# Zero products on TensorE at launch, and a gate and its stores divided once more in the last tile

## The chip, the cores and the metric

One core of one Trainium2 chip. The metric is the time of the whole kernel on the device, in microseconds (us), as the median of several executions. "Granted clock" is the mean TensorE clock in an execution's clock records, 1.0 being full; the time before the first record (19.21 us in the profiled run of before) is counted as full. In these traces TensorE multiplies matrices into PSUM, VectorE and ScalarE work on the products element by element, and SyncE only issues DMA transfers. I call the "clock gate" open where a clock record says 1.0 and shut where it says 0.5; the same product of 128 columns starts every 107 ns before the first record of before and every 55 ns after it.

## The reference

```python
# x: (8, 3072, 256) float32
X = np.fft.rfft(x, axis=1)                       # along the sequence
Yr = Xr @ w_r - Xi @ w_i + b_r                   # complex 256 x 256 product
Yi = Xr @ w_i + Xi @ w_r + b_i
Yr = np.sign(Yr) * np.maximum(np.abs(Yr) - 0.01, 0.0)   # the same for Yi
y = np.fft.irfft(Yr + 1j * Yi, n=3072, axis=1)
# then a channel mix on y, with y_prev = y moved by one token
xk = mu_k * y + (1 - mu_k) * y_prev
xr = mu_r * y + (1 - mu_r) * y_prev
k = np.maximum(xk @ w_k, 0.0)                    # 256 -> 1024
v = k * k @ w_v                                  # 1024 -> 256
out = v / (1 + np.exp(-(xr @ w_r2)))             # the gate
```

## The kernel before

The transforms are done as matrix products. A small scheduler in the kernel's own Python issues everything in an order fixed at build time, and PSUM is four pairs of banks that go round (`take`, `release`). The 8 x 3072 tokens of the channel mix are 48 tiles of 512.

The launch: the first sequence comes in four chunks; `direct` does the first DFT step on each as it lands (L326 in the profile), and `turn` the transposes after it (L344).

```python
def load_x(b, q):
    t = xs_pool.tile([N1, 8, D], BF16, name="xs")
    src = x[b].rearrange("(n1 n2) d -> n1 n2 d", n2=N2)
    nc.gpsimd.dma_start(out=t, in_=src[:, 8 * q:8 * q + 8, :])
    xs[b, q] = t
...
def take():
    f, i = min((f, i) for i, f in enumerate(pair_free) if f is not None)
    pair_free[i] = None
    return banks[:, i, :], i
...
# direct(), chunk q, half c
for i in range(8):
    nc.tensor.matmul(pv[:, i, :], xt[:, i, 128 * c:128 * c + 128], FT, start=True, stop=True)
...
# turn(u)
for i in range(4):
    for c in range(NCD):
        nc.tensor.matmul(ps[:, 256 * i + 128 * c:256 * i + 128 * c + 128],
                         live["X1"][:, c, 4 * u + i].rearrange("p r n -> p (r n)"), ident, ...)
```

The end: the last tile's products (L670), its gate (L681) and its four stores (L692), done in two parts. Every second store of the last tile goes by ScalarE's queue, all others by SyncE's.

```python
            lo, hi = (512 * p, 512 * p + 512) if final else (0, 1024)

            def gated(k):
                nc.vector.tensor_tensor(out=o[:, lo:hi], in0=ps[:, lo:hi], in1=rg[:, lo:hi], op=ALU.mult)
                ...
            def store(k):
                ...
                for xx in range(4):
                    queue = nc.scalar if final and xx % 2 else nc.sync
                    queue.dma_start(out=rows[hh, half, xx][:, lo:hi], in_=o[32 * xx:32 * xx + 32, lo:hi])
```

## Time and profile before

| | before |
|---|---|
| median of 3 runs | 592.51 us (592.41 to 592.64) |
| profiled run, its span | 592.85 us, 591.0 us |
| TensorE busy | 566.1 us (96%) |
| VectorE, ScalarE busy | 522.4 us (88%), 421.0 us (71%) |
| last weight load of TensorE to the span's end | 5.35 us |

### The profile page before, as it was taken

What the parts mean: (1) busy time and instruction counts of PE and PEld (TensorE: products, weight loads), DVE (VectorE), ACT (ScalarE), POOL (GpSimd) and SP (SyncE); (2) the same over time, 40 slices, a digit from 0 to 9 for tenths busy, and PEclk for the clock granted to TensorE, in tenths of its full rate; (3) what the DMA queues carried; (4) which work ended last, traced back from release to release, by engine and by line L of the source; (5) the groups of instructions that cost most, each with busy time, mean ns of one, the idle gap of its engine ahead of it and who ended that gap; (6) DMA issues with size and microseconds to landing.
All of it is one profiled execution on the core that took longest, in us unless ns stands there. A gap on an engine that the chain in (4) does not pass through costs nothing.

```text
span 591.0 us, 12301 instructions
## 1 busy us (share of the span) xinstructions
PE 566.1 (96%) x4822; PEld 429.1 (73%) x4889; DVE 522.4 (88%) x831; ACT 421.0 (71%) x459; POOL 26.7 (5%) x56
## 2 busy tenths in 40 slices
PE   3999999999999999999999999999999999999996
PEld 3888666777767777677777777677876787776665
DVE  7799999789998899898998989988999889979883
ACT  5786967677768677676777677777776867767652
POOL 7101000000000000000000000000000000000000
PEclk9999999999999999999999999999999999999999
DMA  8976978724598265963478655683337722352223
GB/s 134 142 149 161 187 181 231 179 72 106 127 230 234 60 139 143 248 182 78 107 183 245 148 116 130 169 229 107 101 97 232 179 55 73 104 165 71 65 57 94
DMA packets 69594, 84.38 MB, mean 143 GB/s; under 512 B 9121, under 2 KB 54560, under 8 KB 69536
## 3 DMA queue, kind: packets, MB, share of 16 engines
q1 hardware_dynamic: 62912, 68.98, 41.7%
q0 software_dynamic: 6432, 14.36, 16.7%
q8 instruction: 38, 0.62, 0.4%
q10 hardware_dynamic: 192, 0.26, 0.2%
q14 instruction: 20, 0.16, 0.1%
HBM read 50.73 MB, written 47.19 MB: 166 GB/s over the span
## 4 chain that ended last, share of the span: by engine, by line
PE 84%; ACT 6%; DVE 4%; issue 2%; DMA 2%; POOL 0%; SPq 0%; DVEq 0%; POOLq 0%; ACTq 0%
PE banks L670 28%; PE banks L626 24%; PE banks L414 14%; PE banks L653 5%; PE banks L453 4%; PE banks L271 3%; PE banks L386 3%; ACT rl L632 3%; PE banks L534 2%; ACT rg L658 2%; DMA xs<-in_x_dram 1%; PE banks L344 1%; DVE YT L220 1%; DMA out_dram<-o 1%; DVE z L426 1%
## 5 line engine op out<-in xcount | busy, mean ns | idle before, releaser
L632 ACT ACTIVATE rl<-banks 128x1024 bf16<-128x1024 f32 x192 | 193.6, 1029 | 94.3 <-PE banks L626 88.5
L626 PE MATMUL banks<-xk,wk 128*128 128x512 bf16 x701 | 188.7, 379 | 5.3 <-DVE xk L599 0.7
L670 PE MATMUL banks<-wv,k 128*128 128x256 bf16 x1536 | 183.0, 272 | 0.4 <-ACT rl L632 0.3
L670 PEld LDWEIGHTS <-k 128*128 128x128 bf16 x1536 | 149.3, 98 | 29.1 <-issue 1.4
L638 DVE TENSOR_TENSOR k<-rl 128x1024 bf16<-128x1024 bf16 x192 | 130.3, 684 | 13.6 <-ACT rl L632 13.5
L626 PEld LDWEIGHTS <-wk 128*128 128x128 bf16 x768 | 73.9, 98 | 60.7 <-issue 3.1
L414 PEld LDWEIGHTS <-XT 128*128 128x128 bf16 x768 | 74.5, 98 | 16.1 <-DVE XT L396 0.7
L414 PE MATMUL banks<-wi,XT 128*128 128x256 bf16 x384 | 73.3, 273 | 0.1
L414 PE MATMUL banks<-wr,XT 128*128 128x256 bf16 x384 | 73.3, 272 | 0.1
L599 DVE SCALAR_TENSOR_TENSOR xk<-diff,muk,YT 128x512 bf16<-128x512 bf16 x96 | 69.0, 744 | 0.2
L599 DVE SCALAR_TENSOR_TENSOR xr<-diff,mur,YT 128x512 bf16<-128x512 bf16 x96 | 68.7, 744 | 0.0
L681 DVE TENSOR_TENSOR o<-banks,rg 128x1024 f32<-128x1024 f32 (+1 forms) x49 | 58.6, 1195 | 3.7 <-PE banks L670 3.4
L218 ACT ACTIVATE YT<-banks 128x768 bf16<-128x768 f32 x57 | 43.5, 830 | 11.3 <-PE banks L534 7.9
L218 ACT ACTIVATE XT<-banks 128x1024 bf16<-128x1024 f32 (+2 forms) x46 | 43.3, 950 | 10.4 <-PE banks L386 10.4
L653 PE MATMUL banks<-wrm,xr 128*128 128x256 bf16 x384 | 49.8, 272 | 0.1
L658 ACT ACTIVATE rg<-banks 128x1024 bf16<-128x1024 f32 x48 | 49.2, 1025 | 0.0
L431 ACT ACTIVATE z<-banks 128x1024 bf16<-128x1024 f32 x32 | 32.7, 1022 | 19.7 <-PE banks L414 19.6
L653 PEld LDWEIGHTS <-xr 128*128 128x128 bf16 x384 | 37.2, 98 | 11.6 <-issue 0.2
L218 ACT ACTIVATE V<-banks 128x1024 bf16<-128x1024 f32 x35 | 35.9, 1025 | 12.8 <-PE banks L453 12.8
L218 ACT ACTIVATE A<-banks 96x1024 bf16<-96x1024 f32 (+1 forms) x39 | 39.3, 1023 | 7.5 <-PE banks L271 6.2
L593 DVE TENSOR_TENSOR diff<-YT 128x1024 bf16<-128x1024 bf16 x48 | 32.8, 683 | 3.8 <-ACT YT L218 3.8
L220 DVE CAST A<-banks 96x1024 bf16<-96x1024 f32 (+1 forms) x21 | 25.5, 1221 | 11.4 <-PE banks L271 9.4
(90 smaller groups left out, 448.3 us busy)
## 6 DMA issues: line engine op xcount, KB each, us to landing
out_dram<-o SPq DMA_DIRECT2D x188, 128.0 KB, 2.3
xs<-in_x_dram POOLq DMA_DIRECT2D x32, 384.0 KB, 6.5
Vdr<-V SPq DMA_DIRECT2D x192, 64.0 KB, 1.8
V<-Vdr SPq DMA_DIRECT2D x32, 384.0 KB, 7.0
Adr<-A SPq DMA_DIRECT2D x24, 384.0 KB, 5.6
A<-Adr SPq DMA_DIRECT2D x48, 192.0 KB, 4.3
wk<-in_moe_w_k_dram POOLq DMA_DIRECT2D x1, 512.0 KB, 14.1
wv<-in_moe_w_v_dram POOLq DMA_DIRECT2D x1, 512.0 KB, 14.5
```

Of the source, the lines that this page charges most:

```text
L218: nc.scalar.activation(out, in_, AF.Copy, bias=0.0, scale=1.0)
L414: nc.tensor.matmul(o, lhs, w[:, c, :], start=(w is wr and c == 0), stop=(w is wi and c == NCD - 1))
L431: nc.scalar.activation(z, ps, AF.Copy, bias=0.0, scale=1.0)
L593: nc.vector.tensor_tensor(out=df, in0=y, in1=yp, op=ALU.subtract)
L599: nc.vector.scalar_tensor_tensor(out=m[:, c, :], in0=df[:, c, :], scalar=mu[:, c:c + 1], in1=yp[:, c, :], op0=ALU.mult, op1=ALU.add)
L626: nc.tensor.matmul(ps[:, 512 * f:512 * f + 512], wk[:, c, 128 * ff:128 * ff + 128], xk[:, c, :], start=(c == 0), stop=(c == NCD - 1))
L632: nc.scalar.activation(rl, ps, AF.Relu, bias=0.0, scale=1.0)
L638: nc.vector.tensor_tensor(out=k2, in0=rl, in1=rl, op=ALU.mult)
L653: nc.tensor.matmul(ps[:, 256 * q:256 * q + 256], xr[:, c, 128 * q:128 * q + 128], wrm[:, c, :], start=(c == 0), stop=(c == NCD - 1))
L658: nc.scalar.activation(rg, ps, AF.Sigmoid, bias=0.0, scale=1.0)
L670: nc.tensor.matmul(ps[:, 256 * q:256 * q + 256], K2[t][:, ff, 128 * q:128 * q + 128], wv[:, ff, :], start=(ff == 0), stop=(ff == NCF - 1))
L681: nc.vector.tensor_tensor(out=o[:, lo:hi], in0=ps[:, lo:hi], in1=rg[:, lo:hi], op=ALU.mult)
```

## The change

Its intent: TensorE waits for inputs until 6.3 us anyway, so let it multiply zeros in that time, so that its clock gate is open when the first real products come; a few more zero products between the chunks are to keep it open. And at the end, gate and store the last 512 columns as twice 256, so that the last stores start earlier.

```diff
+    idle = const.tile([128, 512], BF16, name="idle")
+    nc.vector.memset(idle, 0.0)
+
+    def keep_warm(ps, n):
+        for _ in range(n):
+            nc.tensor.matmul(ps[:, 0:512], idle[:, 0:128], idle, start=True, stop=True)
@@ direct(), after a chunk's products
+                if b == 0 and c == 1:
+                    spare, i = take()
+                    keep_warm(spare, 2 if q < 3 else 1)
+                    release(i, end + 0.5)
@@ v_unit()
-            lo, hi = (512 * p, 512 * p + 512) if final else (0, 1024)
+            cuts = ((0, 512), (512, 768, 1024))[p] if final else (0, 1024)
             def gated(k):
-                nc.vector.tensor_tensor(out=o[:, lo:hi], in0=ps[:, lo:hi], in1=rg[:, lo:hi], op=ALU.mult)
-                e = run_on("dve", k, 0.7 if final else 1.22)
+                for lo, hi in zip(cuts, cuts[1:]):
+                    nc.vector.tensor_tensor(out=o[:, lo:hi], in0=ps[:, lo:hi], in1=rg[:, lo:hi], op=ALU.mult)
+                    e = run_on("dve", k, 1.22 * (hi - lo) / 1024)
+                    if final:
+                        store(lo, hi)
@@ before the first unit is issued
+    spare, i = take()
+    keep_warm(spare, 14)
+    release(i, 6.0)
```

(Cut: the tiles before the last store as they did.) That is 21 zero products, one memset, one gate and four stores more.

## The prediction

> **What bounds the kernel now.** I read the page first (busy time, then the chain that ended last), then the launch and the end, where the change acts: groups by shape and the order of time for the launch; order of time, waits and landings for the end.
>
> ```profile
> PE 566.1 (96%) x4822; PEld 429.1 (73%) x4889; DVE 522.4 (88%) x831; ACT 421.0 (71%) x459; POOL 26.7 (5%) x56
> ...
> PEclk9999999999999999999999999999999999999999
> ...
> PE 84%; ACT 6%; DVE 4%; issue 2%; DMA 2%; POOL 0%; SPq 0%; DVEq 0%; POOLq 0%; ACTq 0%
> ```
>
> TensorE is busy for 96% of the span and makes up 84% of the chain; the body (from some 25 us to 584 us) gets no instruction from the change. What is left is a launch of some 25 us and an end of some 7 us. The clock row shows full clock everywhere, also at launch. The durations contradict it. Groups by shape, 6 to 20 us, then 20 to 60 us:
>
> ```profile
> L326 PE MATMUL banks<-FT,xs 96*128 96x96 f16 x64 | 5.9, 280 | 2.0 <-DMA xs<-in_x_dram 2.0
> L344 PE MATMUL banks<-ident,YT 128*128 128x128 f16 x48 | 4.9, 289 | 0.8 <-ACT YT L218 0.7
> ```
>
> ```profile
> L326 PE MATMUL banks<-FT,xs 96*128 96x96 f16 x64 | 3.6, 205 | 0.5 <-ACT V L218 0.4
> L344 PE MATMUL banks<-ident,YT 128*128 128x128 f16 x48 | 3.2, 219 | 0.6 <-DVE YT L220 0.6
> ```
>
> The same products take 280 and 289 ns at launch, 205 and 219 ns later. The starts show it too: L344 starts every 107 ns between 15.35 and 19 us, every 55 ns later; L326 every 80 ns, later every 43 ns. The first clock record in the trace stands at 19.2 us (to full); before it the page assumes full clock. So the launch runs at half clock until 19.2 us. The launch in order of time:
>
> ```profile
> 12.64 1.58 ACT L735 ACTIVATE G<-YT,sc 128x1536 f16<-128x1536 f32 x1
> 12.77 1.46 PE L326 MATMUL banks<-FT,xs 96*128 96x96 f16 x16 [0.33 <-DMA xs<-in_x_dram]
> ...
> 14.34 0.96 DVE L220 CAST YT<-banks 128x768 bf16<-128x768 f32 x1 [0.83 <-PE banks L326]
> ...
> 14.81 1.56 ACT L739 ACTIVATE G<-YT,sc 128x1536 f16<-128x1536 f32 x1
> ...
> 17.17 1.94 ACT L218 ACTIVATE A<-banks 128x1024 bf16<-128x1024 f32 x2 [0.80 <-PE banks L344]
> ...
> 19.56 1.02 ACT L218 ACTIVATE A<-banks 128x1024 bf16<-128x1024 f32 x1 [0.45 <-PE banks L344]
> ```
>
> L326 waits for the loads of x (9.11, 10.98 and 12.77 us), which a faster TensorE cannot move. After L344, ScalarE waits twice for TensorE: 0.80 and 0.45 us. The end, in order of time and in the queue's own waits:
>
> ```profile
> 585.15 2.59 ACTq L692 DMA_DIRECT2D out_dram<-o  x4
> 586.12 0.69 DVE L681 TENSOR_TENSOR o<-banks,rg 128x512 f32<-128x512 f32 x1 [1.00 <-PE banks L670]
> ```
>
> ```profile
> SPq L692 <- DMA out_dram<-o: 1.5, 2, 1.3
> ```
>
> The last gate ends at 586.81, but the last store starts only at 588.35 and lands at 590.12; 0.9 us of closing barrier follow. In between the SyncE queue waits 1.3 us for a store to land. The end is therefore set by the store queue, not by the gate.
>
> [...] L344 was dense from 15.35, and the gate opened at 19.2. [...] no trace here has zero operands yet. [...] the built program lets the first quarter gate wait for the same last product as before. [...] here one store costs its queue 0.36 to 0.47 us, which matters when seven queue up.
>
> **The change part by part.** The listing of both built programs shows pure additions: 21 zero products and their weight loads, one memset first on VectorE, one gate more, four stores more. Everything else keeps its order; PSUM pairs only rotate by one.
>
> *Launch, the added products.* 14 products of 512 columns at half clock take some 14 x 427 ns = 6.0 us (512 columns at L344's 128 columns in 107 ns), from about 1.1 us (VectorE is idle until 2.36, so the memset is free) to at most 7.1. If the gate opens on the way, they end before 6.3, when the first real product can start. In the worst case x's first chunk is 0.8 us late, which the wait until 9.11 for the second swallows. The later 2+2+2+1 cost 0.43 us a pair at full clock and lie in the waits for x or ahead of L344.
>
> *Launch, the gain.* Step by step:
> - Third and fourth chunk of L326 still start at 10.98 and 12.77. ScalarE cannot use the gain: L735 waits for VectorE's angles (end 12.60), so L735, the copy at 14.12 and L739 (to 16.37) keep their times. VectorE's copy of the last part starts at 13.65 instead of 14.34 and ends at 14.61.
> - L344 starts at 14.96 and is not held at 15.35. At 55 ns its units of 8 end at 15.57, 16.00, 16.44; then PSUM pairs must come free.
> - ScalarE's A copies now follow L739 back to back: 16.28, 17.20, 18.12 instead of 17.17, 18.09, 19.56. The next, XT0, starts at 19.06 instead of 20.48: **1.4 us** earlier. VectorE (16.83 first copy, four small G pieces, then 17.2 and 18.4) keeps up.
> - From there ScalarE is the chain: XT 19.54, GI 20.28 (was 21.65), VectorE's L396 at about 22.0 (was 23.37), L414 at 22.3 instead of 23.69. Its weights landed by 14.2, the bias at 21.8, ahead of its use at 23.6. The next loads of x, used at 34, landed by 32.3. So the 1.4 us go through to the body, which is a chain of relative times.
>
> *End, the gates.* 1024 columns take 1224 ns and 512 take 692, so 256 take about 160 + 266 = 426 ns. The first quarter is ready at 586.54 (0.27 earlier), the second at 586.97 (0.16 later).
>
> *End, the stores.* Each store takes the next of eight completion semaphores and waits until that one's previous store has landed. In the kernel before, SyncE's second store of part 0 shares one with ScalarE's first store of part 0 (issued 585.15, landed 587.51): it started at 587.53, then 587.94, 588.35. With four stores more the numbering shifts. In the new listing it is already the fourth store of the tile before (old start 585.17, without a wait) that shares with ScalarE's first one. So SyncE stands from 585.1 until that lands, at about 587.2 (estimate: 15 of its 16 parts landed by 587.03, the last at 587.51 beside the store that now waits), and then has **seven** stores to issue instead of three: 0.36 + 5 x 0.43 = 2.5 us to the last start at 589.7, landing some 1.65 later at 591.3 instead of 590.12. The end grows by about **1.2 us** (0.9 if the landing comes at 587.0 and issue is quick, 1.5 if at 587.5).
>
> *Sum.* 592.5 - 1.4 + 1.2 = 592.3 us.
>
> **The rivals.**
> - *The end gains as intended.* If the semaphores don't bind as I read the listing, finer stores overlap better, and the end changes by 0 to -0.4: about 590.9. Against: the 1.3 us wait is measured, and the listing names the same kind of wait one store earlier. I give this 15%.
> - *Zero products don't open the gate, or it closes in the waits for x.* Then the launch gains nothing and the end's loss stays: 593.7. For: no trace has zeros. Against: the waits are at most 1.5 us, and the gate closed at the very end only after a window with 0.3 us of work. 12%.
> - *The launch's gain is eaten later*, by loads at fixed times or by VectorE: 593 to 593.7. Against: each load has 1.7 us or more to spare. 8%.
>
> **Range and chances.** The body cancels and runs scatter by 0.2 us. The launch's part is -1.4 with 0.25 either way, the end's +1.2 with 0.35, together about 0.45; the rivals stretch both sides to 590.9 and 593.7. Centre 592.3, range 590.9 to 593.5. Two per cent are 11.9 us; neither end of the kernel has that much: 0.01, 0.98, 0.01.
>
> **What would show it right or wrong.** L344 at launch at 219 ns a product, with the second start right after 14.96; ScalarE's first A copy at 16.3 and XT0 near 19.1; L414 near 22.3; the last product of TensorE about 1.4 us earlier. Then the time from the last product to the span's end 1.2 us longer than now (586.1 to 591.0, 4.9 us), SyncE waiting some 2 us for a store with seven stores behind. Wrong: L344 still at 289 ns (gate shut); the last product moves by less than 1 us (gain eaten); the time after the last product stays at 4.9 us or shrinks (stores misread).

The sum came to 592.5 - 1.4 + 1.2 = 592.3 us, from times in the trace of before. But that zeros would open the gate was the assumption at that time, and so was that waits of at most 1.5 us would not close it.

What the trace of before shows of the rest: TensorE was busy for all of the 3.86 us from 15.35 us to the opening at 19.21, and for 0.26 of the 3.41 us ahead of the closing at 589.23 (the "window with 0.3 us of work"). The 0.43 us for a pair of zero products agrees with L626, where eight products of 512 columns take 1.73 us. The transfers of SyncE and ScalarE near the end carry eight completion semaphores in turn, numbers 107 to 110 and 115 to 118: ScalarE's first store of part 0 has number 116 and landed at 587.51, and SyncE's second one, which waits for 116, started at 587.53. The last three stores landed 1.67 to 1.82 us after their starts. The "closing barrier" is the time from the last landing, 590.12 us, to the end.

## More of the kernel before

In the body, the inverse transform of each sequence goes through DRAM. Four stores of 64 KB for each `V` tile, then four loads, all by SyncE's queue; the products at L534 use them.

```python
                    for cj in range(4):
                        nc.sync.dma_start(out=Vdr[b][...], in_=vt[32 * cj:32 * cj + 32])
...
                    for q in (2, 3, 0, 1):
                        nc.sync.dma_start(out=V2[b, q], in_=Vdr[b][:, 8 * q:8 * q + 8, :])
```

## The result, and the profile after

| | before | after |
|---|---|---|
| median | 592.51 us (6 runs, 592.27 to 593.49) | 593.36 us (6 runs, 592.65 to 594.13) |
| profiled run, span | 591.0 us | 592.86 us, 591.1 us |

The ratio is 1.0013 (95%: 1.0 to 1.0026). Ratios here are the mean time of one kernel's fast runs over that of the other's fast runs of the same rounds, so not quite the ratio of the medians.

The six runs fall into two groups: 592.65, 592.86 and 592.88 at a granted clock of 0.999, and 593.84, 594.02 and 594.13 at 0.994. The profiled run is one of the first group, so its trace shows the change at its better.

The launch. Two views of after: the groups by shape on TensorE, 6 to 20 us, and the order of time (start, length, engine, line; in brackets the wait ahead of it and what ended it). L326 of before is L334 here, L344 is L356.

```profile
L77 PE MATMUL banks<-idle 128*128 128x512 bf16 x11 | 3.5, 411 | 0.0
L334 PE MATMUL banks<-FT,xs 96*128 96x96 f16 x64 | 3.4, 206 | 2.1 <-DMA xs<-in_x_dram 2.1
L356 PE MATMUL banks<-ident,YT 128*128 128x128 f16 x48 | 3.0, 219 | 1.3 <-ACT YT L226 1.3
```

```profile
14.81 1.56 ACT L756 ACTIVATE G<-YT,sc 128x1536 f16<-128x1536 f32 x1
...
14.97 2.99 PE L356 MATMUL banks<-ident,YT 128*128 128x128 f16 x48 [1.26 <-ACT YT L226]
...
16.28 2.84 ACT L226 ACTIVATE A<-banks 128x1024 bf16<-128x1024 f32 x3
...
18.99 1.32 ACT L226 ACTIVATE XT<-banks 128x512 bf16<-128x512 f32 x2
```

The products run at 206 and 219 ns: the gate is open. The clock records say so too: it opened at 6.03 us, when TensorE had multiplied nothing but zeros (its first other product starts at 6.59). The three copies of A on ScalarE, which stood 0.80 and 0.45 us for TensorE before, now follow one another without a wait, and XT comes at 18.99 instead of 20.48.

The end. One line of before in order of time, then after, then the waits of after's SyncE queue (in total, times, longest):

```profile
583.88 4.96 SPq L692 DMA_DIRECT2D out_dram<-o  x8
```

```profile
582.57 6.20 SPq L709 DMA_DIRECT2D out_dram<-o  x10
...
583.84 3.16 ACTq L709 DMA_DIRECT2D out_dram<-o  x6
584.81 0.76 DVE L695 TENSOR_TENSOR o<-banks,rg 128x256 f32<-128x256 f32 x2 [1.00 <-PE banks L682]
```

```profile
SPq L709 <- DMA out_dram<-o: 1.8, 1, 1.8
```

The gates end 1.25 us earlier than before (585.57 against 586.81). But SyncE stands 1.8 us once for a store to land, from ahead of its fourth store of the tile before; that store started at 585.655, at once after ScalarE's part-0 store had landed at 585.64; both carry semaphore 116 in the trace. Seven stores follow from there, the last starting at 588.34 and landing at 589.92. SyncE's ten stores take 6.20 us where eight took 4.96. Of these 1.24 us only 0.3 are longer waits (1.8 against 1.5); the rest is the issue of two more stores on SyncE (0.41 to 0.52 us from one start to the next). The moved wait and the longer queue come together here, and no run has one without the other.

To see where the time went, I took TensorE's weight loads of the real work, which are the same list in both kernels, and compared when the same load starts in the two traces. That splits the difference of two spans into stretches that add up:

| difference from before, us | launch (to 40 us) | body | of it at 245 to 256 us | end | span |
|---|---|---|---|---|---|
| after | -1.72 | +0.40 | +0.44 | +1.35 | +0.04 |

("End" is from the last weight load to the end of the span.) The launch gains and the end loses about what was expected. The body gives back 0.44 us at one place, near 249 us. Outside it the body of all traces below agrees with before within 0.05 us, save 0.55 us in one (e13), so this method tells tenths of a microsecond apart, where the total times of one kernel scatter by more.

TensorE's waits from 245 to 256 us, of before and then of after (for what, in total, times, longest):

```profile
PE banks L534 <- ACT rl L632: 0.2, 1, 0.2
```

```profile
PE banks L546 <- DMA V<-Vdr: 0.6, 1, 0.6
```

In place of a wait for ScalarE there is one for a load of V.

### The profile page after: what moved, and what is told of

It is laid out like the page before. It is cut to its first block, busy times and chain, and to the rows that moved or that the text cites. A ratio compares the mean times of both kernels' runs of the same rounds, so it can differ in the third digit from the quotient of the medians.

```text
span 591.1 us, 12417 instructions
## 1 busy us (share of the span) xinstructions
PE 572.3 (97%) x4910; PEld 427.2 (72%) x4910; DVE 522.4 (88%) x833; ACT 421.0 (71%) x459; POOL 26.4 (4%) x56
## 4 chain that ended last, share of the span: by engine, by line
PE 80%; ACT 7%; DVE 5%; DMA 4%; issue 2%; SPq 1%; POOL 1%; DVEq 0%; POOLq 0%; ACTq 0%
PE banks L682 26%; PE banks L638 23%; PE banks L426 14%; PE banks L665 5%; PE banks L465 4%; PE banks L398 3%; PE banks L279 3%; ACT rl L644 2%; PE banks L546 2%; ACT rg L670 1%; DMA Adr<-A 1%; DMA Vdr<-V 1%; ACT YT L226 1%; DMA out_dram<-o 1%; DMA V<-Vdr 1%
## 5 line engine op out<-in xcount | busy, mean ns | idle before, releaser
L638 PE MATMUL banks<-xk,wk 128*128 128x512 bf16 x768 | 193.2, 379 | 2.0 <-DVE xk L611 0.7
L426 PEld LDWEIGHTS <-XT 128*128 128x128 bf16 x768 | 74.5, 98 | 15.9 <-DVE XT L408 0.4
L426 PE MATMUL banks<-wr,XT 128*128 128x256 bf16 x384 | 73.3, 272 | 0.1
L426 PE MATMUL banks<-wi,XT 128*128 128x256 bf16 x384 | 73.3, 273 | 0.0
L695 DVE TENSOR_TENSOR o<-banks,rg 128x1024 f32<-128x1024 f32 (+2 forms) x50 | 58.6, 1174 | 3.7 <-PE banks L682 3.4
```

The costliest lines, as they stand in the source:

```text
L426: nc.tensor.matmul(o, lhs, w[:, c, :], start=(w is wr and c == 0), stop=(w is wi and c == NCD - 1))
L638: nc.tensor.matmul(ps[:, 512 * f:512 * f + 512], wk[:, c, 128 * ff:128 * ff + 128], xk[:, c, :], start=(c == 0), stop=(c == NCD - 1))
```

## The experiments

Theory: (1) the gain at launch comes from the open gate; (2) the loss at the end comes from the number of stores, which moves a shared completion semaphore to an earlier store and lengthens the queue behind it, not from the divided gate; (3) the slower group of runs is the gate closing again between the chunks. Rivals: the gate opens no better with zeros than with any short instruction; the divided gate itself delays; the slower runs come from elsewhere. All results were correct against the reference.

| run | what differs | median us (runs) | ratio to before (95%) | launch | at 245 to 256 | end |
|---|---|---|---|---|---|---|
| e1 | launch part alone | 591.75 (5) | 0.9984 (0.9971-0.9996) | -1.36 | +0.60 | -0.02 |
| e2 | end part alone | 594.3 (4) | 1.0025 (1.0009-1.004) | -0.18 | +0.38 | +1.40 |
| e3 | e2 with only stores divided | 594.21 (4) | 1.0028 (1.0015-1.0042) | +0.17 | 0.00 | +1.51 |
| e4 | e2 with only the gate divided | 593.05 (4) | 1.0006 (0.9992-1.002) | +0.06 | 0.00 | +0.01 |
| e5 | e1, five zero products after each chunk | 591.54 (5) | 0.9982 (0.997-0.9994) | -1.51 | +0.17 | -0.16 |
| e6 | e1, none after the chunks | 592.65 (4) | 0.9998 (0.9984-1.0013) | -0.27 | +0.93 | -0.09 |
| e9 | e5 and stores on both queues | 591.57 (6) | 0.999 (0.9974-1.0006) | -0.91 | +1.32 | -0.52 |
| e10 | the changed kernel again | 593.22 (5) | 1.0019 (1.0005-1.0032) | -1.70 | 0.00 | +1.36 |
| e11 | e1, products of one column | 592.82 (4) | 1.0008 (0.9994-1.0022) | -0.01 | 0.00 | -0.06 |
| e12 | e1, twice as many of half the size | 592.48 (5) | 0.9997 (0.9984-1.0009) | -0.28 | 0.00 | -0.02 |
| e13 | e12 and stores on both queues | 592.3 (5) | 1.0001 (0.9989-1.0014) | -0.03 | 0.00 | -0.58 |

The last three columns split the profiled run of each, as above. e1 to e4 share a chip (before there: 592.52 us, 591.44 to 593.18), e5 to e9 another (592.5), e10 to e13 a third (592.5). e7 is told below.

### e1: the launch alone

```diff
-            cuts = ((0, 512), (512, 768, 1024))[p] if final else (0, 1024)
+            cuts = ((0, 512), (512, 1024))[p] if final else (0, 1024)
```

> The launch half of the change alone (21 zero products, end as before). Theory: launch gains 1.3 to 1.4 us and nothing else changes, so runs at mean clock 0.999 take about 591.2; runs at mean clock 0.994, where the clock gate closed once more during the launch, lose that gain again and take about 592.4. Two groups are expected, near half and half. Rival (part of the gain is eaten later in the body): good runs at 592 or more. Rival (the two groups come from the end of the kernel): one group only.

591.75 us, ratio 0.9984. The launch part alone is a gain of about 0.9 us in the mean. Its end is that of before (-0.02), so the loss there belongs to the end part. Two groups of runs, half and half, were expected and did not show: one run of five has a clock of 0.995, and with 591.86 us it is no slower than the others (591.16 to 592.08). SyncE's waits of e1 are those of before, 1.5 us in two waits:

```profile
SPq L709 <- DMA out_dram<-o: 1.5, 2, 1.3
```

### e2, e3, e4: the end alone, and its two halves

e2 has no zero products; e3 gates the 512 columns at once and stores twice 256; e4 gates twice 256 and stores 512.

```diff
 # e2, against the changed kernel
-    idle = const.tile(...)   and every keep_warm
 # e3, against e2
             def gated(k):
+                lo, hi = cuts[0], cuts[-1]
+                nc.vector.tensor_tensor(out=o[:, lo:hi], ...)
                 for lo, hi in zip(cuts, cuts[1:]):
-                    nc.vector.tensor_tensor(out=o[:, lo:hi], ...)
                     if final:
                         store(lo, hi)
 # e4, against e2
-                    if final:
-                        store(lo, hi)
+                if final:
+                    store(cuts[0], cuts[-1])
```

> The end half of the change alone (second part gated and stored in two, no zero products). Theory of shared store semaphores: SyncE's fourth store of the tile before waits until ScalarE's first store of part 0 has landed, seven stores queue behind, 1.2 to 1.4 us more than before: about 593.8, one group at the clock of before. Intent of the change: 592.5 or less, down to 592.1.

> End only: one gate of 512 columns as before, but its stores cut into two halves (four stores more). Theory of the stores: the listing lets the fourth store of the tile before wait for the first of that tile (landed 585.8 before) and part 0's second store on SyncE for ScalarE's second; the last store starts near 589.4 and the time is about 593.5 (+1.0). Rival, that the gate's division costs the time: 592.5 as before.

> End only: two gates of 256 columns, stores as before (one set for both). Theory of the stores: the second gate ends 0.16 us later than the one of before, but SyncE's queue stands until 587.5 anyway, so 592.5 as before, within 0.2. Rival, that the gate's division costs the time: 593.8 as the end-only kernel.

SyncE's waits for stores at the end, of e2, e3 and e4:

```profile
SPq L699 <- DMA out_dram<-o: 1.9, 1, 1.9
```

```profile
SPq L700 <- DMA out_dram<-o: 2.2, 3, 1.2
```

```profile
SPq L699 <- DMA out_dram<-o: 1.5, 2, 1.3
```

With the stores divided the end grows by 1.40 and 1.51 us; with the gate alone divided it stays (+0.01), and e4's time is that of before within its interval. So the divided gate is free, and the stores cost it all. e3's end was expected to grow by 1.0 us, so half a microsecond of it was missed; SyncE waits three times for landings, 2.2 us in all. Which store waits for which is the expectation's reading of the listing; the lines above don't tell it. e4 in order of time shows the two quarter gates in the place of the one of 0.69 us:

```profile
586.18 0.76 DVE L685 TENSOR_TENSOR o<-banks,rg 128x256 f32<-128x256 f32 x2 [1.00 <-PE banks L672]
```

### e5 and e6: more zero products between the chunks, and none

```diff
 # e5, against e1
-                    keep_warm(spare, 2 if q < 3 else 1)
+                    keep_warm(spare, 5)
 # e6, against e1
-                if b == 0 and c == 1:
-                    spare, i = take()
-                    keep_warm(spare, 2 if q < 3 else 1)
-                    release(i, end + 0.5)
```

> Launch half alone, with five zero products after every chunk of x instead of 2, 2, 2, 1. Theory: the changed kernel's runs at mean clock 0.994 are runs in which [...] the gate closed again; with TensorE filled between the chunks every run keeps 0.998 or more, the recorded half-clock stretch inside the launch never comes, and launch gains 1.3 us or more in all runs: about 591.2. Rival (the 0.994 runs have another cause): the same share of 0.994 runs as before.

> Launch half alone, with the 14 products at the start but none between the chunks of x. Theory: the gate opens near 6 us and closes again before L344 in nearly all runs, mean clock 0.994 or so, opening again near 18 to 22 us; the launch's gain of 1.3 us is lost nearly whole, some 592.3. Rival (the 14 products are enough): clock 0.999 and 591.2.

e6 is back at the time of before, with a granted clock of 0.991 to 0.994 in all four runs. Its trace is the one that shows the gate closing. Clock records: opened at 4.75 us, closed at 11.57, opened at 18.40, so 6.82 and 6.83 us apart. The records of before are 570.03 us apart (19.21 to 589.23), those of after 583.68 us (6.03 to 589.71). All four are whole multiples of 3.413 us (2, 2, 167 and 171), which I take as the step by an estimate from these four, and call a window. Stretches of e6 cut at those windows (from and to; length; busy time of TensorE, its weight loads, VectorE, ScalarE, GpSimd with counts; then clock, DMA share, GB/s):

```profile
4.75:8.16 3.41, 2.25 (x24) 1.25 (x21) 2.91 (x11) 1.54 (x3) 3.12 (x10) 1.00 0.90 158
8.16:11.57 3.41, 1.63 (x32) 1.42 (x32) 3.28 (x6) 1.95 (x4) 3.26 (x5) 1.00 1.05 206
11.57:14.98 3.41, 1.55 (x19) 1.26 (x17) 2.68 (x3) 2.93 (x4) 1.66 (x3) 0.50 1.27 124
14.98:18.40 3.42, 3.42 (x32) 3.28 (x33) 1.79 (x6) 2.77 (x3) 0.63 (x2) 0.50 1.09 28
```

TensorE was busy for 1.63 of the 3.41 us of the second window, and the gate closed at its end; it opened again after the fourth, fully busy one. e6's TensorE in order of time:

```profile
8.90 0.85 PE L334 MATMUL banks<-FT,xs 96*128 96x96 f16 x16 [1.74 <-DMA xs<-in_x_dram]
10.80 0.85 PE L334 MATMUL banks<-FT,xs 96*128 96x96 f16 x16 [1.04 <-DMA xs<-in_x_dram]
12.63 1.46 PE L334 MATMUL banks<-FT,xs 96*128 96x96 f16 x16 [0.98 <-DMA xs<-in_x_dram]
14.97 4.54 PE L352 MATMUL banks<-ident,YT 128*128 128x128 f16 x48 [0.88 <-ACT YT L226]
```

The fourth chunk takes 1.46 us instead of 0.85, and the transposes 4.54 instead of 2.99. No wait was longer than 1.74 us. So waits that short closed the gate here, where they left TensorE busy for 48% of a window. In the changed kernel's profiled run the thinnest window up to 16.3 us was 63% busy (2.15 of 3.41 us), and the gate stayed open.

What this says of the slower group: 6.83 us at half clock lower the mean by 0.5 x 6.83 / 591 = 0.006, to 0.994, just the granted clock of that group. The closing at the end of every run explains no more than 0.003 (e2 closes 3.7 us before its end and has 0.997). That group is 1.2 us slower (594.0 against 592.8 in the mean), and e6 lost about as much of the launch (1.1 us against e1). No run of that group was itself profiled, so this is an inference from the clock, and from e6. The profiled run's own trace allows it: laid elsewhere, from 11.55 to 14.96 us, a window finds TensorE busy for only 1.57 of 3.41 us (46%), no more than the one that closed the gate in e6; in e5 the same stretch is busy for 3.16 us. Where the windows fall differs between runs: the gate opened at 6.03 us in after, 5.87 in e10 and 6.95 in e5. By my count on after's trace, about a fifth of the possible places have a window as thin as e6's, and half have one below 55%.

e5, with five zero products, had 0.998 to 1.0 in all five runs; its time is the lowest median of all, but it is not shown to be faster than e1 (0.9982 against 0.9984 of before).

### e7, e9: the last tiles' stores on both queues

```diff
-                    queue = nc.scalar if final and xx % 2 else nc.sync
+                    queue = nc.scalar if t >= NT - 2 and xx % 2 else nc.sync
```

e7 is before with this edit, e9 is e5 with it. It takes stores of the tile before off SyncE, so that SyncE would not stand ahead of them.

> The kernel before with one edit: the stores of the tile before the last are dealt over both queues too, so that no store of the last tile shares its completion semaphore with one that is still under way. Theory: the last store starts near 587.2 instead of 588.35 and the end shrinks by 1.1 us, about 591.4. Rival (transfer, not the queue, sets the end): 592.5 as before.

> Five fillers at launch and the even queues at the end, last tile divided as in the kernel before. Theory: -1.35 at launch and -1.1 at the end add up: about 590.1, all runs at clock 0.998 or more. If the loads of V near 250 us eat part of the launch's gain as they did by 0.4 to 0.65 us in two profiles, up to 590.7.

e7 gave no answer. The run that was profiled took 3388.68 us. Its page:

```profile
PE 3312.9 (98%) x4822; PEld 1533.6 (45%) x4889; DVE 542.6 (16%) x831; ACT 452.6 (13%) x459; POOL 26.3 (1%) x56
```

The same 4822 products took 3312.9 us instead of 566.1 while VectorE stayed near its 522. That trace has no clock record, so its page shows full clock. The other three runs took 592.12, 595.86 and 591.54 us (ratio 1.001, 0.9985 to 1.0035). Why, is not known; the same program did it in one of four runs, so the edit alone does not explain it. e9's end is 0.52 us shorter, about half of what I had hoped for: SyncE still stood once for a store to land, for 0.5 us. Its runs scatter from 590.71 to 594.41 us, and the total gains nothing over e5: 591.57 us, where 590.1 to 590.7 were expected.

### e10: the changed kernel again

No edit.

> The changed kernel unaltered, on another chip. Theory of the gate: two groups again, runs at clock 0.998 or more near 592.8, runs at 0.995 or less near 594.0, the second in a third to two thirds of the runs. Theory of the body: the loss between 245 and 256 us (0.44 us in the first profile) is there again, 0.3 to 1.3 us. Rival for both (accidents of one chip): one group, no loss in the body.

593.22 us, ratio 1.0019, on another chip: the first result is repeated. One of the five runs has the clock of 0.994 (593.86 us), so the gate closed in about 4 of all 11 runs. A run of 594.82 us at 0.997 is not explained by it. The profiled run repeats launch and end within 0.02 us, but loses nothing at 249 us, where 0.3 to 1.3 us had been expected: that loss is not a fixed cost of the change.

### e11: zero products of one column

```diff
-            nc.tensor.matmul(ps[:, 0:512], idle[:, 0:128], idle, start=True, stop=True)
+            nc.tensor.matmul(ps[:, 0:1], idle[:, 0:128], idle[:, 0:1], start=True, stop=True)
```

> The launch half alone with products of 1 column in place of 512: the same 42 instructions for TensorE, too short to open the gate. Theory of the body: the loss at 245 to 256 us comes from the 42 more instructions, which move the 16 KB instruction load that lies behind SyncE's four stores of V (1.6 us after the first of them in the kernel before, 0.3 us ahead of it in the changed one) into them; so here launch 0, body +0.4 to +0.9, end 0: 592.9 to 593.4, with one of the four stores taking 1 us or more. Rival (the body's loss comes from the earlier start): 592.5, no loss.

The same number of instructions as e1, and the launch is that of before (-0.01). Groups by shape of e11, 6 to 20 us:

```profile
L334 PE MATMUL banks<-FT,xs 96*128 96x96 f16 x64 | 5.9, 280 | 1.8 <-DMA xs<-in_x_dram 1.8
L356 PE MATMUL banks<-ident,YT 128*128 128x128 f16 x48 | 5.1, 298 | 0.8 <-ACT YT L226 0.8
```

The gate stayed shut; the first clock record stands at 19.49 us. So the same number of products opened it with 512 columns (at 6.03 us in after) and not with one: here it was the time that TensorE spent on them, and the launch's gain is the gate's. The loss of 0.4 to 0.9 us that was expected at 249 us did not come.

### e12, e13: twice as many zero products of 256 columns

The loss at 249 us: SyncE issues four stores of V (0.44 to 0.51 us apart in before), GpSimd issues a load of x (384 KB) 1.8 us after the first of them, and the first load of V waits for the last store (landed at 237.91 and started at 238.03 us in before, 239.23 and 239.34 in after). In the traces with zero products of the changed count, a 16 KB load of the queue that brings instructions falls in or near those four (0.3 us ahead of the first in after, 1.62 us behind it in before); one store's issue then takes 0.96 to 1.5 us instead of 0.38 to 0.46. The last store falls behind the load of x and lands 7.2 to 7.8 us after the first, not 4.3 to 4.6. (In e5 the 16 KB load comes before all four stores, which start late: the load of x follows the first after 0.7 us, and the last store lands 6.5 us after it.) With 42 instructions more on TensorE the load came 1.9 us earlier against the first store. I took it that the number of instructions places it, an estimate from these two traces, so I changed the number: 28 and 10 products of half the size.

```diff
-            nc.tensor.matmul(ps[:, 0:512], idle[:, 0:128], idle, start=True, stop=True)
+            nc.tensor.matmul(ps[:, 0:256], idle[:, 0:128], idle[:, 0:256], start=True, stop=True)
-                    keep_warm(spare, 2 if q < 3 else 1)
+                    keep_warm(spare, 10)
-    keep_warm(spare, 14)
+    keep_warm(spare, 28)
```

e13 has the queue edit of e7 as well.

> Launch half alone, 28 products of 256 columns at the start and 10 after each chunk: 136 more instructions instead of 42, gate filled as with five of 512. Theory of the body: the instruction load moves some 6 us earlier (1.9 us for 42 instructions) and so past the four stores of V; launch -1.4 to -1.7, body 0 to +0.1, end 0: about 591.0, all runs at clock 0.998 or more. Rival: the body loses 0.4 or more whatever the number.

> The same launch, and the stores of the tile before the last dealt over both queues. In the disturbed profile of the even queues with five fillers the end shrank by 0.5 us instead of 1.1[...]. So launch -1.5, body 0, end -0.5: about 590.5, best of all. Rival (body loses as in the five-filler kernel): 591.2.

The last store of V now landed 3.2 us after the first started, and the wait for V at 249 us was gone, as expected. But up to 40 us e12 gained only 0.28 us and e13 0.03, and their times, 592.48 and 592.3 us, miss the expected 591.0 and 590.5. e12's TensorE in order of time:

```profile
21.30 0.38 PE L426 MATMUL banks<-wr,XT 128*128 128x256 bf16 x2
23.00 0.38 PE L426 MATMUL banks<-wi,XT 128*128 128x256 bf16 x2 [1.32 <-issue]
```

TensorE stood 1.32 us for nothing that the profile shows ("issue"), in the midst of one run of products. The first 16 KB instruction load in the trace had started at 20.57 us (before: 22.25), beside data loads whose packets took 107% of the 16 DMA engines' time from 18 to 24 us. My guess is that TensorE stood for instructions; the trace does not show it. e13 has such a stop of 1.57 us in the same place, and e9 one of 0.98 us at 25.2. Ahead of these stops nothing was lost: L381, the first product after the transposes, starts at 18.25 to 18.29 us in all seven traces with an open gate there (after, e1, e5, e9, e10, e12, e13) and at 19.81 in before. So the open gate is worth 1.5 us, and what the launch column shows less is lost behind it. In e13 a wait for V came back near 321 us (0.8 us), the 0.55 us named above. So the cost seems to have moved from one place to another. And it must be said against the account of 249 us that e10 and e11 also have the late stores, with V's first load as late, and lost 0.00 there, and that e2, whose stores were in time, lost 0.38. The landings tell which load counts: in after, e1, e2, e5, e6 and e9 the wait ends about 0.05 us after the last of V's four loads has landed. The first load started at 239.34 us in after and at 239.36 in e10, but the last landed at 249.26 in after and at 248.64 in e10, just in time. Why the last load varies is not settled.

## Why the prediction was right or wrong

The class (within 2%) and the range (590.9 to 593.5) held: 593.36 us. The centre, 592.3, was 1.1 us low, and that the range held is in part luck: three of the six runs lie above it, and the median falls between the two groups, where no run lies. By its steps:

- **The gate opens with zeros.** Right: open at 6.03 us, real products at 206 and 219 ns. In e11 products of one column left it shut (L334 at 280 ns).
- **The launch's chain.** Right nearly to the digit: L356 at 14.97 (predicted 14.96) without a stop, first A copy at 16.28 (16.28), XT at 18.99 (19.06), GI at 20.16 (20.28), and the first product that needs L408's XT (L426) at 21.97 (22.3). Gain 1.72 us against 1.4. In all traces with the gate open it is 1.5 us at L381; what is left of it at 40 us varies, from 1.72 to 0.03 us, largely with the stops told under e12.
- **The divided gates.** Right: 0.42 us each (426 ns predicted), free in e4.
- **The semaphores.** Right in mechanism: one wait of 1.8 us (predicted about 2) ahead of the fourth store of the tile before, then seven stores. In the time of before, with after's last product 1.31 us earlier, the wait ended at 586.97 (predicted 587.2) and the last store started at 589.65 (589.7). It landed 1.58 us later, not 1.65. The landing moved by 1.11 us against the last product; the other 0.24 of the +1.35 is the closing, where SyncE checks the completion semaphores one by one: after the last landing one check was left in before (at 590.14 us), five in after (589.94 to 590.18, 0.06 us apart). Predicted +1.2, measured +1.35, so the close agreement owes something to the closing, which had been left at its old 0.9 us. e2, e3 and e4 confirm that the stores cost it, not that the moved wait alone does.
- **"So the 1.4 us go through to the body, which is a chain of relative times."** This step failed, in part. Between 40 and 245 us it held to 0.02 us. Near 249 us, 0.44 us went to a wait for V in the profiled run, 0.00 in e10, up to 1.32 in e9. The prediction gave 8% to "the launch's gain is eaten later" and looked at the loads of x at launch alone, not at loads later: the instruction load near 232 us came 1.9 us earlier against V's stores in after.
- **The rival "or it closes in the waits for x", 12%.** I treated it as all or nothing and argued that the waits, at most 1.5 us, were too short, which no trace had shown. Yet it came in about 4 of 11 runs, by the granted clock, at some 1.2 us each; in e6 waits up to 1.74 us sufficed, with a window only 48% busy. The median of six runs falls between the two groups, (592.88 + 593.84) / 2 = 593.36. This is the term that was missing from the sum: the good runs alone are at 592.8.

The sum in the profiled run: -1.72 + 0.40 + 1.35 = +0.03 us (+0.04 unrounded), against -0.2 predicted.

What would be kept: the zero products with five after each chunk (e5, ratio 0.9982 to before), and the end as it was. That is about 1.0 us better than before, while the changed kernel is 0.8 to 1.1 us slower than before. These ratios come from different chips, each against before on the same chip; no larger gain was found.

## What to carry to other kernels

Filling TensorE's idle time at launch with products of zeros paid here only where the windows of 3.41 us up to the dense work stayed filled: at 63% busy the gate stayed open (after), at 48% it closed (e6), though no wait was over 1.74 us. So count the busy share of each window, not the longest wait. Before dividing a store in order to start it earlier, see which queue issues it and whose landing each store must await: four stores more cost here 1.4 us, while the divided gate was free. And even this change, confined to the ends, went with an instruction load that came 1.9 us earlier against the stores of V near 232 us, so compare the traces stretch by stretch before trusting a total.
